# Moving the first batch's loads of u to SyncE's queue and the loads of W1 to ScalarE's

## Chip, cores, metric

One core of a Trainium2 chip runs the whole program. The time is device microseconds of one execution. Runs are fast within 1.5% of the fastest. Medians are quoted for each kernel beside the kernel before on the same chip. A few runs of the kernel before stand far off the rest (1189.03, 1190.59, 1190.67 and 1193.23 among values near 1180.5) and still count as fast, so for effects of one microsecond I read medians, lowest values and traces, and take the ratios only as a bound. Each kernel has one trace, of one run. The "granted clock" of a run or stretch is the share of TensorE's full clock that the profile shows for it.

## The reference

```python
scores = (1.0 / S) * np.matmul(z, z.transpose(0, 2, 1))      # B = 8, S = 3008, d_qk = 64
attn   = np.maximum(scores, 0.0) ** 2
x      = (u * np.matmul(attn, v)).reshape(B * S, 256)
h      = x @ w_in                                             # 256 -> 2048
g      = h * (1.0 / (1.0 + np.exp(-1.702 * h)))
return (g @ w_out).astype(np.float32)                         # 2048 -> 256
```

## The kernel before

Attention goes by query blocks of 512 (six chunks per batch; the last has 448). `attend` yields steps of matmuls, and between them the main loop issues loads, casts and other work by tables of (block, step). Scores go to PSUM (`sc`), ScalarE applies the relu (`rl`, three buffers), VectorE squares (`a`), and SyncE turns squared blocks by DMA transpose (`tt`) so that the upper half of the symmetric score matrix serves for the lower one. `u` arrives as `uq`, VectorE turns it (`ut`), and at a block's end the product with `ut` gives `xt`, the input of the up-projection (`hg`, the product with W1). W1 arrives in four quarters in float32 (`wst`, two buffers), and ScalarE casts each to half precision.

```python
    def load_u(b, i):
        eng = pool if b or i else sp
        ...                                   # four DMAs of 32 partitions each
    def load_w(k):
        if k == 0:
            hold = const.tile([P, 1], F16, name="hold")
            pool.tensor_copy(hold, XT[0, 1][:, 0, :1])
        if k < 4:
            WS[k] = pw.tile([P, NCC, DFF // 4], F32, name="wst", tag="y")
            pool.dma_start(WS[k], moe_w_in...[:, :, k * DFF // 4:(k + 1) * DFF // 4])
        ...
    def cast_w(k):
        act.activation(W1[:, :, k * DFF // 4:(k + 1) * DFF // 4], WS.pop(k), AF.Copy, scale=1.0)
    ...
    TURN0 = {(i, (38, 28)[i] if i < 2 else NJ + 4 if i < NCH - 1 else 12): i for i in range(NCH)}
    LOAD0 = {(1, 14): 2, (2, 12): 3, (2, NJ + 20): 4, (4, 8): 5}
    LOADW = {
        (2, 16): 0, (2, 30): 1, (3, 9): 2, (3, 41): 3, (4, 28): 4, ...
    }
    CASTW = {(3, 8): 0, (3, 40): 1, (4, 8): 2, (4, 14): 3}
```

`TURN0` says where VectorE turns which chunk of u, `LOAD0` where u is loaded, `LOADW` where W1's quarters are, `CASTW` where they are cast; NJ is 24.

Of the kernel before, what the change touches and what calls it, by code (L numbers as in the profile page):

```python
# [10 lines left out]
F16 = mybir.dt.float16  # L11
P = 128
# [3 lines left out]
def kernel(  # L16
# [18 lines left out]
    DFF = moe_w_in.shape[1]  # L35
# [8 lines left out]
    NCC = D // P  # L44
# [11 lines left out]
    dve, act, pe, sp, pool = nc.vector, nc.scalar, nc.tensor, nc.sync, nc.gpsimd  # L56

    const = ctx.enter_context(tc.tile_pool(name="const", bufs=1))
# [18 lines left out]
    ZP, WS = {}, {}  # L77
    late, LATE = [], []
    ZT, V16, UQ, UT, XT, unit, TT = {}, {}, {}, {}, {}, {}, {}
# [41 lines left out]
    def first_cast(g, by_act=False):  # L121
        m = g % CB * CB
        for c in range(2):
            dst, src = ZT["st"][g // CB][:, m:m + CB, c, :], ZT["f"][g // CB][:, m:m + CB, :]
            if by_act:
                act.activation(dst, src, AF.Copy, scale=1.0)  # L126
            else:
                dve.tensor_copy(dst, src)

    def first_zt(g):  # L130

        z2 = ZT["st"][g // CB][:, g % CB * CB:(g % CB + 1) * CB]
        zp = ZP[g] if g in ZP else ps1.tile([P, CB, P], F16, name="zp", tag="ps1")
        for k in range(CB):
            pe.transpose(zp[:, k, :], z2[:, k, :, :], ident)  # L135

        def copies():
            zt = ZT[0][:, g * CB:(g + 1) * CB, :].rearrange("d n p -> d (n p)")
            nb = CB if g < NCH - 1 else CB - 1
            dst = zt[:, :nb * P].rearrange("d (p n) -> d p n", n=nb)  # L140
            src = zp[:, :nb, :].rearrange("d n p -> d p n")
            if g in (0, 2, 3):
                act.activation(dst, src, AF.Copy, scale=1.0)  # L143
            else:
                dve.tensor_copy(dst, src)
            if nb < CB:
                dve.tensor_copy(zt[:, nb * P:], zp[:, nb, :])

        return copies


    def load_z(b):
        ZT[b] = pz.tile([P, NJ, P], F16, name="ZT", tag="ZT")
        for n0 in range(0, NJ, NU):
            zst = pw.tile([P, NU, 2, DQK], F16, name="zst", tag="y")
            full = min(NU, NJ - 1 - n0)
            src = z[b, n0 * P:(n0 + full) * P].rearrange("(n p) d -> p n d", p=P)
            pool.dma_start(zst[:, :full, 0, :], src)
            if full < NU:
                for h in range(2):  # L160
                    pool.dma_start(zst[h * SREM:(h + 1) * SREM, full, 0, :], z[b, S0:S])
            pool.tensor_copy(zst[:, :, 1, :], zst[:, :, 0, :])
            sp.dma_start_transpose(ZT[b][:, n0:n0 + NU], zst.rearrange("p n c d -> p (n c d)"))
# [21 lines left out]
    def width(i):  # L185
        return CH if i < NCH - 1 else LAST

    def load_u(b, i):
        eng = pool if b or i else sp
        n = width(i)  # L190
        uq = pu.tile([P, CH // QW, QW, NCC], F32, name="uq", tag="uq")
        src = u[b, i * CH:i * CH + n].rearrange("(q t) c -> t q c", t=QW)
        for k in range(P // QW):
            cs = slice(k * NCC * QW, (k + 1) * NCC * QW)
            eng.dma_start(uq[k * QW:(k + 1) * QW, :n // QW].rearrange("t q c k -> t q (c k)"), src[:, :, cs])  # L195
        UQ[b, i] = uq

    def turn_u(b, i):
        n = width(i)
        ut = pu.tile([P, NCC, CH // QW, QW], F32, name="ut", tag="ut")  # L200
        UT[b, i] = ut
        dve.transpose(
            ut[:, :, :n // QW, :].rearrange("p k q t -> p q k t"),
            UQ.pop((b, i))[:, :n // QW].rearrange("p q c k -> p q k c"),
        )
# [114 lines left out]
    def full(b):  # L320

        return NCH - 2 if b < B - 1 else NCH - 1
# [106 lines left out]

    def load_w(k):  # L430

        if k == 0:
            hold = const.tile([P, 1], F16, name="hold")
            pool.tensor_copy(hold, XT[0, 1][:, 0, :1])
        if k < 4:
            WS[k] = pw.tile([P, NCC, DFF // 4], F32, name="wst", tag="y")
            pool.dma_start(WS[k], moe_w_in.rearrange("(p k) f -> p k f", k=NCC)[:, :, k * DFF // 4:(k + 1) * DFF // 4])
        else:
            fs = slice((k - 4) * CB, (k - 3) * CB)
            pool.dma_start(W2[:, fs], moe_w_out.rearrange("(fo p) c -> p fo c", p=P)[:, fs])  # L440

    def cast_w(k):
        act.activation(W1[:, :, k * DFF // 4:(k + 1) * DFF // 4], WS.pop(k), AF.Copy, scale=1.0)  # L443
# [197 lines left out]
    def take(b, n):  # L641
        for post_ in scores(b, [queue.pop(0) for _ in range(n)]):
            post_()

    def fill(b):
        assert not queue
        queue.extend(u_ for i in range(NCH) for u_ in pieces(b, i))
# [24 lines left out]
    keep_warm(1)  # L672
    copies()
    ZP[3] = ps1.tile([P, CB, P], F16, name="zp", tag="ps1")
    load_u(0, 1)

    for b in range(B):
        nup = NCH * NFG
        more = b + 1 < B
        sched = SCHED0 if b == 0 else SCHED if more else SCHED_LAST  # L680
        turn, load = (TURN, LOAD) if b else (TURN0, LOAD0)
        head = 0
        for i in range(NCH):
            host = b + 1 if more and i == NCH - 1 else b
            if host > b:
                fill(host)
                LATE.append(host)
            for n, step in enumerate(attend(b, i, b == 0 and i < 2)):
                if b == 0 and i == 0 and n == 5:
                    load_u(0, 0)  # L690
                if b == 0 and i == 0 and n == 2:
                    copies = first_zt(3)
                if b == 0 and i == 0 and n == 3:
                    copies()
                if b == 0 and i == 0 and n in FIRST_CAST:
                    first_cast(FIRST_CAST[n], True)
                if b == 0 and i == 0 and n in FIRST_ZT:
                    first_zt(FIRST_ZT[n])()
                if (i, n) in turn:
                    turn_u(b, turn[i, n])  # L700
                if i == 3 and n in (3, 26) and LAST2:
                    LAST2.pop(0)()
                if (i, n) in load:
                    load_u(b, load[i, n])
                if b == 0 and (i, n) in CASTW:
                    cast_w(CASTW[i, n])
                if b == 0 and (i, n) in LOADW:
                    load_w(LOADW[i, n])
                if more and (i, n) == (NCH - 2, 2 if b else 16):
                    load_z(b + 1)  # L710
                if b == 0 and i == NCH - 1 and n in (8, 30, 42):
                    wsums.pop(0)()
                take(host, sched[i].get(n, 0))
                if i == full(b) and n >= HEAD and (n - HEAD) * LAGY // (2 * NJ - 10) >= head and head < LAGY:
                    up_group(b, head)
                    head += 1
                step()
        late.sort(key=lambda t: t[0])
        if more:
            for i in range(2):  # L720
                load_u(b + 1, i)
            for n0 in range(0, NJ, VB):
                load_v(b + 1, n0)
        prods = products(b)
        for q in range(head, nup):
            if more and q in (head + 14, head + 20):
                k = int(q == head + 20)
                turn_u(b + 1, k)
                load_u(b + 1, k + 2)
            up_group(b, q)  # L730
            if b == 0 and q == head + 3:
                wsums.pop(0)()
            product(b, *prods.pop(0))
            if q >= 30 and q % 2 and late:
                late.pop(0)[1]()
        steps = [lambda kp=kp: product(b, *kp) for kp in prods]
        for step in steps:
            step()
            for sum_ in [SUMS.pop(0) for _ in range(min(len(SUMS), 1 + (len(SUMS) > 4)))]:
                sum_()  # L740
            for _, turn_it in [late.pop(0) for _ in range(min(len(late), 1 + (len(steps) < 10)))]:
                turn_it()
        LATE.clear()
        if more:
            while late:
                late.pop(0)[1]()
            take(b + 1, 2)
# [30 lines left out]
```

## Time and profile before

| | kernel before |
|---|---|
| median of 6 runs | 1180.49 us (1180.28 to 1183.42) |
| span of the profiled run | 1178.7 us |
| TensorE time lost against its pace, 40 to 60 and 60 to 80 us | 0.50 and 0.93 us |

The prediction shows the page's main lines. The columns of the timeline are start, length, engine, line, operation, tiles and shapes, count, idle time before it and what ended that. In the timeline (start, length, engine, line, operation, tiles and shapes, count, idle time before it and what ended that), VectorE turns u of chunk 3 with no wait:

```profile
58.81 0.63 DVE L270 TENSOR_TENSOR a<-rl 128x896 f16<-128x896 f16 x1 [0.18 <-ACT rl L256]
59.36 1.24 DVE L202 STREAM_TRANSPOSE ut<-uq 128x1024 f32<-128x1024 f32 x1
```

And TensorE goes from block 3 into the first up-projection (`hg`) without a hole:

```profile
62.53 1.15 PE L358 MATMUL o<-a,V 64*128 64x512 f16 x6
63.52 1.03 PE L399 MATMUL hg<-xt,W 128*128 128x512 f16 x4
```

The trace gives for each transfer when it was issued and when it landed. "Hole" is, throughout, the start of one matmul less the start of the one before and less its regular pace (0.216 us for a 512-column matmul of 128 rows, half that for one of a pair of 64 rows). In the lines, SPq and ACTq are the instructions by which SyncE and ScalarE issue transfers, and `<-` in the brackets names what ended the idle time.

### The profile page before, as it was taken

How to read it: one execution, taken by the hardware profiler on the slowest of the kernel's cores; microseconds unless marked ns; L12 is line 12 of the kernel's file. 1: busy time of each engine (PE TensorE's matmuls, PEld its weight loads, DVE VectorE, ACT ScalarE, POOL GpSimd, SP SyncE). 2: the span in 40 equal slices, each digit the busy share in tenths (PEclk: the TensorE clock that was granted, in tenths of full speed). 3: DMA queues.
4: the chain of work that ended last, by engine and by line, in shares of the span. 5: the costliest groups of instructions: out<-in, count | busy, mean ns of one | idle time of the engine just before them, and what ended most of it. 6: DMA issues, size and time to landing. Idle time of an engine off the chain costs nothing.

```text
span 1178.7 us, 23495 instructions
## 1 busy us (share of the span) xinstructions
PE 1172.5 (99%) x9238; PEld 667.2 (57%) x9238; DVE 870.7 (74%) x1455; ACT 849.6 (72%) x1033; POOL 222.1 (19%) x313
## 2 busy tenths in 40 slices
PE   9999999999999999999999999999999999999998
PEld 3446664466644675446654467544674446744566
DVE  6779866878758786587875878658786587764776
ACT  7888874688746887478864787647876478772785
POOL 5243101231012310132101431014100241001000
PEclk9999999999999999999999999999999999999999
DMA  9998679877698677976879668896578965796023
GB/s 226 217 120 125 133 116 160 91 112 135 106 156 100 108 135 130 150 91 95 147 128 149 94 93 157 139 137 94 94 135 135 141 106 97 127 158 127 1 37 73
DMA packets 449696, 143.66 MB, mean 122 GB/s; under 512 B 414640, under 2 KB 443056, under 8 KB 449584
## 3 DMA queue, kind: packets, MB, share of 16 engines
q1 hardware_dynamic: 392160, 99.80, 51.2%
q0 software_dynamic: 56064, 41.04, 23.1%
q8 instruction: 72, 1.18, 0.4%
q10 hardware_dynamic: 1360, 1.31, 0.4%
q14 instruction: 40, 0.33, 0.1%
HBM read 60.29 MB, written 24.64 MB: 72 GB/s over the span
## 4 chain that ended last, share of the span: by engine, by line
PE 99%; ACT 1%; issue 0%; DVE 0%
PE o L358 40%; PE hg L399 27%; PE st L523 23%; PE sc L235 6%; PE st L526 1%; PE yp L497 1%; PE w L99 0%; ACT rl L256 0%; ACT W L443 0%; ACT gf L407 0%; PE zp L135 0%; ACT ZT L143 0%; ACT zst L126 0%; DVE y L544 0%; DVE nil L75 0%
## 5 line engine op out<-in xcount | busy, mean ns | idle before, releaser
L407 ACT ACTIVATE gf<-hg 128x1024 f32<-128x1024 f32 (+1 forms) x384 | 385.5, 1004 | 113.6 <-PE hg L399 98.3
L256 ACT ACTIVATE rl<-sc 128x1024 f16<-128x1024 f32 (+1 forms) x301 | 287.5, 993 | 145.4 <-PE sc L235 101.2
L358 PEld LDWEIGHTS <-V 64*128 64x128 f16 (+1 forms) x4052 | 217.7, 94 | 253.9 <-issue 11.8
L399 PE MATMUL hg<-xt,W 128*128 128x512 f16 (+1 forms) x1408 | 354.6, 374 | 0.2
L358 PE MATMUL o<-a,V 64*128 64x512 f16 (+3 forms) x2240 | 296.0, 368 | 0.0
L411 DVE TENSOR_SCALAR gt<-gf 128x1024 f16<-128x1024 f32 (+1 forms) x288 | 203.0, 705 | 114.0 <-ACT gf L407 112.8
L195 POOL DMA_DIRECT2D uq<-in_u_dram x188 | 125.2, 674 | 751.8 <-PE sc L235 527.5
L270 DVE TENSOR_TENSOR a<-rl 128x1024 f16<-128x1024 f16 (+1 forms) x266 | 177.6, 670 | 112.3 <-ACT rl L256 111.0
L358 PE MATMUL o<-tt,V 64*128 64x512 f16 (+1 forms) x1510 | 232.2, 377 | 0.0
L399 PEld LDWEIGHTS <-W 128*128 128x128 f16 x1536 | 149.4, 98 | 125.6 <-issue 2.6
L523 PEld LDWEIGHTS <-WT 128*128 128x128 f16 x1472 | 139.1, 98 | 45.1
L523 PEld LDWEIGHTS <-W 128*128 128x128 f16 x1104 | 104.7, 98 | 32.2
L235 PE MATMUL sc<-ZT 64*128 64x512 f16 (+3 forms) x688 | 115.5, 357 | 0.5 <-ACT ZT L143 0.3
L409 ACT ACTIVATE gt<-gf 128x1024 f16<-128x1024 f32 (+1 forms) x96 | 98.9, 1030 | 3.0
L540 ACT ACTIVATE y<-st 128x256 f32<-128x256 f32 x192 | 70.8, 369 | 35.7 <-PE st L523 29.2
L523 PE MATMUL st<-gt,WT 128*128 128x256 f16 (+1 forms) x736 | 91.9, 268 | 0.0
L523 PE MATMUL st<-s,WT 128*128 128x256 f16 (+1 forms) x736 | 90.8, 268 | 0.0
L523 PE MATMUL st<-gt,W 128*128 128x256 f16 (+1 forms) x736 | 90.8, 268 | 0.0
L544 DVE SCALAR_TENSOR_TENSOR y<-st,y 128x256 f32<-128x256 f32 (+1 forms) x144 | 57.7, 407 | 24.3 <-ACT y L540 11.7
L375 DVE TENSOR_TENSOR xt<-o,ut 128x512 f16<-128x512 f32 x80 | 51.3, 683 | 28.5 <-PE o L358 28.5
L477 DVE TENSOR_TENSOR s<-s,gt 128x1024 f16<-128x1024 f16 (+1 forms) x96 | 63.7, 663 | 1.1
L475 DVE TENSOR_TENSOR s<-gt 128x1024 f16<-128x1024 f16 (+1 forms) x96 | 63.3, 660 | 0.0
(59 smaller groups left out, 668.5 us busy)
## 6 DMA issues: line engine op xcount, KB each, us to landing
uq<-in_u_dram POOLq DMA_DIRECT2D x156, 128.0 KB, 3.6
out_dram<-yo SPq DMA_DIRECT2D x156, 128.0 KB, 2.8
V<-in_v_dram POOLq DMA_DIRECT2D x35, 256.0 KB, 6.4
tt<-a SPq DMA_TRANSPOSE x232, 3.4
uq<-in_u_dram POOLq DMA_DIRECT2D x32, 112.0 KB, 5.4
out_dram<-yo SPq DMA_DIRECT2D x28, 96.0 KB, 6.0
wst<-in_moe_w_in_dram POOLq DMA_DIRECT2D x4, 512.0 KB, 6.2
vst<-in_v_dram SPq DMA_DIRECT2D x3, 512.0 KB, 5.4
```

What stands on the lines that cost most here:

```text
L195: eng.dma_start(uq[k * QW:(k + 1) * QW, :n // QW].rearrange("t q c k -> t q (c k)"), src[:, :, cs])
L235: pe.matmul(sc[:, r, :q1 - q0], zt[h, 2 * kp + r, :], zt[h].rearrange("d n p -> d (n p)")[:, q0:q1], start=True, stop=True,)
L256: act.activation(rl[:, :, :n], sc[:, :, :n], AF.Relu, scale=csc)
L270: dve.tensor_tensor(a[:, :, :n], rl[:, :, :n], rl[:, :, :n], ALU.mult)
L358: ins = pe.matmul(acc[c][:, :n], V16[b][h, j].rearrange("p (c k) -> p k c", k=NCC)[:, c], weights(b, i, j)[h], start=(k, m) == first[c], s ...
L399: pe.matmul(hg[:, e, :n], W1[:, c, ff * P:(ff + 1) * P], XT[b, i][:, c, :n], start=(c == 0), stop=(c == NCC - 1),)
L407: act.activation(gf[:, :, :n], hg[:, :, :n], AF.Gelu_apprx_sigmoid, scale=1.0 / FSC)
L409: act.activation(g, gf[:, :, :n], AF.Copy, scale=FSC)
L411: dve.tensor_scalar(g, gf[:, :, :n], FSC, None, ALU.mult)
L477: dve.tensor_tensor(s_, ST[b, k, "S1", h], a11, ALU.subtract)
L523: pe.matmul(bank, right[:, ff], lhs()[:, f], start=first, stop=last, skip_group_check=True)
L540: act.activation(y[:, c, :, o], bank, AF.Copy, scale=1.0 / FSC)
```

## The change

Its intent: in the first batch Pool issues no loads of u or W1. SyncE issues u of all chunks and ScalarE the four quarters of W1; the small copy that only held Pool back goes.

```diff
     def load_u(b, i):
-        eng = pool if b or i else sp
+        eng = pool if b else sp
...
     def load_w(k):
-        if k == 0:
-            hold = const.tile([P, 1], F16, name="hold")
-            pool.tensor_copy(hold, XT[0, 1][:, 0, :1])
         if k < 4:
             WS[k] = pw.tile([P, NCC, DFF // 4], F32, name="wst", tag="y")
-            pool.dma_start(WS[k], ...)
+            act.dma_start(WS[k], ...)
...
     ZP[3] = ps1.tile([P, CB, P], F16, name="zp", tag="ps1")
-    load_u(0, 1)
...
-                if b == 0 and i == 0 and n == 5:
-                    load_u(0, 0)
+                if b == 0 and i == 0 and n in (5, 24):
+                    load_u(0, n // 24)
```

More of the change, by code (lines that the diff above doesn't have):

```diff
@@ L430, in load_w @@
     def load_w(k):
-        if k == 0:
-            hold = const.tile([P, 1], F16, name="hold")
-            pool.tensor_copy(hold, XT[0, 1][:, 0, :1])
         if k < 4:
             WS[k] = pw.tile([P, NCC, DFF // 4], F32, name="wst", tag="y")
-            pool.dma_start(WS[k], moe_w_in.rearrange("(p k) f -> p k f", k=NCC)[:, :, k * DFF // 4:(k + 1) * DFF // 4])
+            act.dma_start(WS[k], moe_w_in.rearrange("(p k) f -> p k f", k=NCC)[:, :, k * DFF // 4:(k + 1) * DFF // 4])
         else:
```

## The prediction

> **What bounds the kernel now.** First the engines' busy time and the chain of waits on the profile page, to learn whether any engine but one matters:
>
> ```profile
> PE 1172.5 (99%) x9238; PEld 667.2 (57%) x9238; DVE 870.7 (74%) x1455; ACT 849.6 (72%) x1033; POOL 222.1 (19%) x313
> ...
> PE 99%; ACT 1%; issue 0%; DVE 0%
> ```
>
> TensorE is busy 1172.5 of 1178.7 us, and the chain that ended last runs through it for 99%. So a gain must come from TensorE's remaining holes, and a loss must open a new hole in it. Second, the list of waits, where the largest wait of all is just the one that the change takes away:
>
> ```profile
> POOL uq L195 <- PE sc L235: 527.5, 14, 66.1
> POOL wst L437 <- PE sc L235: 13.1, 2, 8.3
> POOL wst L437 <- ACT W L443: 3.0, 1, 3.0
> PE w L99 <- DVE nil L75: 1.2, 1, 1.2
> PE sc L235 <- ACT ZT L143: 0.3, 1, 0.3
> ```
>
> The reader should see that the first three belong to Pool, which nobody on the chain waits for, and that TensorE's own two waits sum to 1.5 us, both before 6 us. Third, only the first batch changes, so the busy times by stage there (columns: stretch, length, then busy us of TensorE, weight loads, VectorE, ScalarE, Pool, granted clock, DMA share, GB/s):
>
> ```profile
> 38.00:52.00 14.00, 14.00 (x134) 6.37 (x130) 10.04 (x16) 11.79 (x13) 4.23 (x7) 1.00 1.21 223
> 52.00:64.00 12.00, 12.00 (x111) 5.91 (x106) 9.29 (x17) 11.61 (x15) 1.81 (x3) 1.00 1.12 198
> 64.00:80.00 16.00, 15.76 (x73) 6.81 (x72) 11.15 (x19) 13.99 (x14) 6.48 (x9) 1.00 1.02 117
> ```
>
> Here are the two things that can hurt: ScalarE is 97% busy in 52 to 64 us (11.61 of 12.00), and the DMA engines are at or over a full share in all of it. Busy hides small delays, so I also took the starts of consecutive matmuls from the trace and compared them with their regular pace (0.216 us for a full 512-column one, half of that for each of a pair of 64-row ones). What is lost over 20 us is 5.2 us in 0 to 20 (start-up), 2.3 in 20 to 40 (a 0.2 us step at each change between 64-row and 128-row tiles), 0.5 in 40 to 60 and 0.9 in 60 to 80; later it is about 0.35 on average. The single holes in 40 to 80 us are 0.25 at 54.2, 0.21 at 56.7, and 0.28 each at 68.9 and 72.0 us. The last two wait for the casts of W1's third and fourth quarters on ScalarE; those quarters landed long before or (68.90 against 71.41 us for the cast) 2.5 us before. No load is what is waited for.
>
> **The Trainium skill.** "Trainium Kernel Development and Optimization", Key Constraints: DMAs from the SP, ACT and POOL queues run on the same 16 DMA engines, and spreading them saves only the sequencer's issue time. That agrees with the shares above, over 1.0 already: the move changes no bytes. "DMA: Bandwidth & Descriptors", Anatomy of one DMA: a semaphore wait happens on the issuing sequencer before dispatch, not in the DMA engine. So a load put on ScalarE makes ScalarE wait; the trace shows it on Pool, whose third W1 load stood 3.0 us until the cast of the first. "Perfetto Trace Analysis", DVE / Act Engine Instruction: compute instructions go into a wait queue and an execution FIFO while the sequencer goes on. So an issue of about 0.5 us can lie beneath an ACTIVATE of 1.0 us; nothing in the kernel before shows this in the middle of a stage.
>
> **The change, part by part.** (1) Removed from Pool: 20 u loads of 0.65 us, one 0.19 us copy (`hold`) and 4 W1 loads of 0.71 us, 16 us in all. The chain has none of it, so it is worth 0.
>
> (2) Added to SyncE: 20 u loads (five chunks of four). The four already there took 0.48 us each:
>
> ```profile
> 14.19 2.16 SPq L195 DMA_DIRECT2D uq<-in_u_dram  x4
> 16.45 45.97 SPq L298 DMA_TRANSPOSE tt<-a  x20
> ```
>
> Each chunk is thus 2.2 us more of a queue that stands in order and is nearly always occupied in 16 to 62 us; four chunks fall into or beside it, 8.6 us. Against it stands the slack of the transposes: from the trace, the tile for key chunk 2 of block 0 landed at 26.7 and is first read by TensorE at 38.9; the others have 8.3, 18.0, 14.5, 8.4, 14.4, 13.4, 13.5, 10.1 and 10.7 us. The queue also had gaps (19.2 to 25.6 us, waiting for VectorE), which swallow the first moved chunk, and Pool's loads no longer compete with it at 17 to 30 us. Delays of 2 to 6 us fit; 0 on the path. The tightest u is chunk 3: VectorE turned it at 59.36; I put its new issue at about 54 and its landing at 57.5 to 60.5. VectorE may wait up to about 1 us; ScalarE has three `rl` buffers and would feel it only after about 1.5 us.
>
> (3) Added to ScalarE: 4 issues of about 0.5 us (its two v loads took 0.47 and 0.57). Where they stand decides. In the changed program the first comes after the ACTIVATE that ended at 42.12; the next begins at 44.11 after idling 2.0 us, so it is free. The second comes about 46.9, beneath or behind an ACTIVATE. The slack of TensorE there (start of its next scores less the end of the ACTIVATE that frees their PSUM tile) is 0.39 to 0.71 us. Free or nearly. The third and the fourth each follow a cast:
>
> ```profile
> 44.11 8.53 ACT L256 ACTIVATE rl<-sc 128x1024 f16<-128x1024 f32 x9 [2.00 <-PE sc L235]
> 52.54 1.05 ACT L443 ACTIVATE W<-wst 128x1024 f16<-128x1024 f32 x1
> 53.48 8.18 ACT L256 ACTIVATE rl<-sc 128x1024 f16<-128x1024 f32 x9
> 61.56 1.05 ACT L443 ACTIVATE W<-wst 128x1024 f16<-128x1024 f32 x1
> 62.51 0.91 ACT L256 ACTIVATE rl<-sc 128x896 f16<-128x896 f32 x1
> 63.31 0.49 ACT L251 ACTIVATE rl<-sc 128x384 f16<-128x384 f32 x1
> 63.82 1.28 ACT L407 ACT_TABLE_LOAD   x1
> ```
>
> The fourth load waits in the program for the end of the cast just ahead of it, at 62.61. With the issue, the next ACTIVATE begins at about 63.15 in place of 62.51. It frees the PSUM tile of the first up-projection, which started at 63.52 with 0.10 us of slack: TensorE loses about 0.64 - 0.10 = 0.5 us. The third waits for the cast that ended at 53.59, while the next ACTIVATE already runs to 54.5; beneath it there is room for the issue, if its other wait is over.
>
> (4) That other wait is the new thing. In both programs the transfers of SyncE and ScalarE share eight completion semaphores in rotation, and each issue waits until the earlier user of its semaphore has landed. In the changed program one semaphore is used in turn by W1's first quarter (ScalarE), the first half of the transpose for block 1 and key chunk 4 (SyncE), the third quarter (ScalarE) and the fourth. So the in-order queues now wait for each other. First quarter: issued about 42.2 and landing, at the 5.5 to 7.3 us of the four before, at 48 to 49.5. The transpose, which went out at 46.15 before, now goes at 48.5 to 50 and lands, at its 4.9 us of before, at 53.4 to 54.8. The third quarter is ready to go at 53.6. ScalarE stands between 0 and 1.2 us; the slack of TensorE there is 0.05 to 0.07 us, so nearly all passes on. I take 0.4. The fourth needs the third landed, at about 54.2 + 6.3 = 60.5, before its turn at 62.6: fits with 2 us.
>
> Sum: 0 - 0 + 0.5 (fourth load) + 0.4 (semaphore) + 0.1 (second) = +1.0, less at most 0.3 if a hole at 54 to 57 closes, for which I take 0.2. From the median 1180.45 that is 1181.2 us. The other seven batches stay: their orders on each engine are the same.
>
> **Rivals.** A: Pool's descriptors or its late loads were in the way of the transposes or of VectorE, and the early stage gets quicker. For it: DMA share 1.08 to 1.23 in 16 to 52 us and transposes that took up to 8.9 us to land. Against it: TensorE never waited for a transpose. At most the holes of 40 to 60 us, 0.5 us: 1180.0. B: the cross-wait bites, ScalarE stands 2 us or more at 54, u of chunk 3 comes late, and both pass to TensorE: +3 to +4, 1184. It needs the first quarter to land at 51 or later; the slowest W1 load before took 7.3 us, which gives 49.5. C: ScalarE's issues are hidden wholly and the semaphore wait is met: 1180.4. I hold C and my sum about equally likely, B at one in eight.
>
> **Range and chances.** All rivals lie within 0.3% of the time before, whose own three runs spread over 3 us (1180.28 to 1183.42). 1179.6 to 1184.2 should hold it 8 times in 10. For 2% TensorE would have to lose or gain 24 us; it has only about 9 us of holes in the first 80 us, most of them start-up, so faster is all but excluded, and slower by so much would take ScalarE or SyncE standing for 24 us.
>
> **What would show it.** Pool has no load before about 69 us. The first W1 issue on ScalarE stands in an idle stretch near 42; the fourth near 62.6 and TensorE's first up-projection begins 0.5 us later against its neighbours. If the transpose named above goes out right after W1's first quarter lands, step 4 is right; if ScalarE's third issue starts more than 1 us after the cast's end, B is. Wrong would be: TensorE waiting for a transposed tile, VectorE waiting over 1.5 us for u, or any change after 100 us.

## The result

The changed kernel takes 1182.08 us in the median of 6 runs (1181.40 to 1184.67), the kernel before 1180.49: 1.6 us more. The ratio of the fast runs is 1.0012, with a 95% interval of 0.9999 to 1.0025. (Ratios are the mean time of one kernel's fast runs over that of the other's of the same rounds, so not quite the ratio of the medians.) The profiled run was the slowest of the six, at 1184.67; its span is 1182.9 us, 4.2 us over the one before.

The page's first lines and chain, after:

```profile
PE 1173.7 (99%) x9238; PEld 667.8 (56%) x9238; DVE 871.2 (74%) x1455; ACT 849.6 (72%) x1033; POOL 205.4 (17%) x288
...
PE 97%; ACT 1%; DMA 1%; DVE 0%; issue 0%; SPq 0%; DVEq 0%; ACTq 0%
```

Pool lost 16.7 us of work, as planned, and TensorE's share of the chain fell from 99 to 97%: a transfer and SyncE's queue have come into it. By stage (columns as in the prediction):

```profile
52.00:64.00 12.00, 11.39 (x104) 5.55 (x101) 6.92 (x12) 9.95 (x12) 0.00 (x0) 1.00 1.15 195
64.00:80.00 16.00, 14.24 (x57) 5.77 (x57) 9.94 (x16) 12.64 (x14) 2.44 (x3) 0.89 0.97 150
```

TensorE lost 0.6 us in the first of these and 1.5 more than before in the second, where its granted clock fell to 0.89. The lists of waits, SyncE's own and that of the other engines, name the new ones (who waited, for whom, us in all, times, longest):

```profile
SPq L298 <- DMA wst<-in_moe_w_in_dram: 6.4, 1, 6.4
DVE ut L202 <- DMA uq<-in_u_dram: 3.6, 1, 3.6
ACT rl L256 <- DVE a L270: 2.2, 1, 2.2
PE hg L399 <- ACT rl L256: 2.1, 1, 2.1
```

Read upwards, TensorE's first up-projection waited for ScalarE's relu to free its PSUM tile, ScalarE for VectorE to free an `rl` buffer, VectorE for u of chunk 3; and earlier SyncE had stood 6.4 us for W1's first quarter. The timelines show the same by the clock, first SyncE, then VectorE, ScalarE and TensorE:

```profile
36.76 17.96 SPq L298 DMA_TRANSPOSE tt<-a  x8
54.77 3.75 SPq L195 DMA_DIRECT2D uq<-in_u_dram  x4
```

```profile
58.53 0.63 DVE L270 TENSOR_TENSOR a<-rl 128x896 f16<-128x896 f16 x1 [0.18 <-ACT rl L256]
62.71 1.25 DVE L202 STREAM_TRANSPOSE ut<-uq 128x1024 f32<-128x1024 f32 x1 [3.56 <-DMA uq<-in_u_dram]
```

```profile
53.20 1.02 ACT L256 ACTIVATE rl<-sc 128x1024 f16<-128x1024 f32 x1
53.33 0.56 ACTq L434 DMA_DIRECT2D wst<-in_moe_w_in_dram  x1
...
61.27 1.05 ACT L440 ACTIVATE W<-wst 128x1024 f16<-128x1024 f32 x1
62.35 0.55 ACTq L434 DMA_DIRECT2D wst<-in_moe_w_in_dram  x1
64.56 0.92 ACT L256 ACTIVATE rl<-sc 128x896 f16<-128x896 f32 x1 [2.23 <-DVE a L270]
```

```profile
62.24 1.15 PE L358 MATMUL o<-a,V 64*128 64x512 f16 x6
65.52 1.86 PE L399 MATMUL hg<-xt,W 128*128 128x512 f16 x4 [2.13 <-ACT rl L256]
67.18 1.06 PE L358 MATMUL o<-a,V 128*128 128x512 f16 x2
```

The hole is 2.30 us. After it four matmuls took 1.86 us where they took 1.03 before: eight of them in a row were 0.43 us apart, twice the pace, which is 1.65 us more. In the stretch from 66 to 69 us the granted clock is 0.52:

```profile
66.00:69.00 3.00, 3.00 (x9) 1.03 (x8) 2.18 (x6) 2.18 (x2) 0.00 (x0) 0.52 1.23 192
```

So this profiled run lost 2.30 + 1.65 = 3.95 us of its 4.2. (What is left is small and lies elsewhere: TensorE began 0.3 us earlier than before, and lost 0.4 at about 1084 us, where it waited 0.2 us for a transposed tile. The second run of this kernel, e1, has no such loss; e3, e6 and e12 have 0.3 to 0.7 us at the same matmul.)

The Trainium skill, "TensorE: Matmul & The Clock Gate", What's actually happening, says that the array falls to half its clock after at least one idle window of about 3.4 us, and that the windows are free-running: they do not start with the kernel. The traces agree with the half clock and with the windows, and not with the length of idling. The half clock lasted from 65.45 to 68.86 us, 3.41 us, and began 61.44 us after the clock's first change, both in this run and in e1; in the other traces the next change came after 1170.77 or 1174.18 us. These are 18, 343 and 344 times 3.413 us, so the changes stand on a grid whose place differs from run to run. In the grid's window from 62.04 to 65.45 TensorE was idle for 2.05 us in all (by the profile's modelled ends), not for the whole of it; in e1 it was 2.27. Idle sums of 1.84 us in one window (e2) and of 1.76 (e10, whose hole was longer but lay across two windows, 1.11 and 1.76) were not followed by half clock. So in these four traces what tells is how much idle time falls into one window; no experiment moved it on purpose.

The five other runs, 2 to 3 us faster and with a mean clock of 0.999 or 1.000 against 0.998, presumably paid the hole and not the half clock.

### The profile page after: what moved, and what is told of

It is laid out like the page before. It is cut to its first block, busy times and chain, and to the rows that moved or that the text cites. A ratio compares the mean times of both kernels' runs of the same rounds, so it can differ in the third digit from the quotient of the medians.

```text
span 1182.9 us, 23487 instructions
## 1 busy us (share of the span) xinstructions
PE 1173.7 (99%) x9238; PEld 667.8 (56%) x9238; DVE 871.2 (74%) x1455; ACT 849.6 (72%) x1033; POOL 205.4 (17%) x288
## 3 DMA queue, kind: packets, MB, share of 16 engines
q10 hardware_dynamic: 2448, 3.41, 1.1%
## 4 chain that ended last, share of the span: by engine, by line
PE 97%; ACT 1%; DMA 1%; DVE 0%; issue 0%; SPq 0%; DVEq 0%; ACTq 0%
PE o L358 39%; PE hg L399 27%; PE st L520 23%; PE sc L235 6%; PE st L523 1%; PE yp L494 1%; ACT rl L256 0%; DMA uq<-in_u_dram 0%; DMA tt<-a 0%; PE w L99 0%; SPq L195 0%; DVE a L270 0%; ACT W L440 0%; ACT gf L407 0%; DVE xt L375 0%
## 5 line engine op out<-in xcount | busy, mean ns | idle before, releaser
L411 DVE TENSOR_SCALAR gt<-gf 128x1024 f16<-128x1024 f32 (+1 forms) x288 | 200.0, 694 | 115.0 <-ACT gf L407 112.6
L195 POOL DMA_DIRECT2D uq<-in_u_dram x168 | 111.1, 668 | 752.0 <-PE sc L235 543.1
```

The costliest lines, as they stand in the source:

```text
L195: eng.dma_start(uq[k * QW:(k + 1) * QW, :n // QW].rearrange("t q c k -> t q (c k)"), src[:, :, cs])
L411: dve.tensor_scalar(g, gf[:, :, :n], FSC, None, ALU.mult)
```

## The experiments

All ran with five timed rounds. The theory at the start: SyncE stands for W1's first quarter through a shared completion semaphore, so u of chunk 3 comes late, and the delay passes down through VectorE and ScalarE to TensorE. R1: SyncE's queue is too long with u, semaphores or not. R2: ScalarE's own issues are the cost. In the table, "hole" is the one ahead of the first up-projection (0.00 in the kernel before), of the profiled run, and "u 3" is when the last load of chunk 3's u landed.

| run | median us | before | difference | by lowest values | hole us | u 3 landed |
|---|---|---|---|---|---|---|
| changed kernel | 1182.08 | 1180.49 | +1.6 | +1.1 | 2.30 | 62.5 |
| e1_again | 1182.34 | 1180.75 | +1.6 | +1.6 | 2.47 | 62.6 |
| e2_w_alone | 1183.79 | 1180.75 | +3.0 | +2.9 | 0.75, and 2.35 at 55 us | 56.0 (from Pool) |
| e3_u_alone | 1181.30 | 1180.75 | +0.5 | 0.0 | 0.31 | 61.5 |
| e4_turn_late | 1181.52 | 1180.75 | +0.8 | +1.2 | 0.74 | 62.2 |
| e6_u3_early | 1181.52 | 1180.86 | +0.7 | +0.8 | 1.42 | 41.4 |
| e7_w0_early | 1181.24 | 1180.86 | +0.4 | +0.7 | 0.74 | 55.9 |
| e8_cast_early | 1181.14 | 1180.86 | +0.3 | +0.1 | 0.42 | 62.7 |
| e10_cast_only | 1182.29 | 1180.86 | +1.4 | +1.2 | 3.03 | 63.5 |
| e12_both | 1180.50 | 1181.33 | -0.8 | +0.3 | 0.00 | 55.3 |
| e17_pool_cast | 1179.59 | 1181.33 | -1.7 | -0.7 | 0.00 | 55.7 |

The kernel before was disturbed in the last call (five of its eleven runs over 1182; its lowest is 1180.20), so e12 and e17 are better held against its lowest. All ratios' intervals contain 1: the smallest and the largest ratio are 0.9977 (0.9944 to 1.0010, e17) and 1.0027 (0.9995 to 1.0059, e2). No ratio is clear of the noise; the causes below rest on the holes in the traces, with the medians beside them.

### e1_again: the changed kernel, unaltered

> The changed kernel once more, unaltered. All theories: +0.8 to +2.0 us over the kernel before in the fast runs. What it is for: a second profile, because the first was of the slowest of six runs (1184.67 against a median of 1182.08). My theory (SyncE stands for W1's first quarter through a shared completion semaphore, so u of chunk 3 comes late, so VectorE, ScalarE and TensorE stand one after the other): u of chunk 3 lands again after 60 us, VectorE waits 1.5 to 3.6 us for it, TensorE's first up-projection is 1 to 2.3 us late; in a run near the median without the slow matmuls of half pace that followed the hole in the first profile. Rival R2 (the fourth W1 issue on ScalarE itself costs it): the hole is 0.5 to 0.7 us and VectorE's wait does not matter.

The same 1.6 us, and the same picture: VectorE waited 3.7 us, the hole was 2.47 us, and half pace followed it again in the profiled run (1184.28 us, clock 0.998). One unprofiled run of the six was also at 1184.44 with that clock. So the first profile was no accident, but it shows the dearer of two outcomes.

### e2_w_alone: W1 from ScalarE, u left on Pool

```diff
-        eng = pool if b else sp
+        eng = pool if b or i else sp
+    load_u(0, 1)
-                if b == 0 and i == 0 and n in (5, 24):
-                    load_u(0, n // 24)
+                if b == 0 and i == 0 and n == 5:
+                    load_u(0, 0)
```

> W1's quarters from ScalarE, u of all chunks but 0 still from Pool. My theory: u of chunk 3 comes from Pool's own queue in time, so at most the half microsecond of the fourth issue is left: 0.0 to +0.7 us over before. Rival R1 (SyncE's queue is too long with the u loads, semaphores or not): 0.0. Rival R2 (ScalarE's issues are the cost): +1.2 to +2.0 us, all of the loss.

This part alone costs 3.0 us, more than the whole change: my figure, R1's and R2's all failed. ScalarE's timeline shows why. Its third W1 issue stood from the cast's end to 56.12, and the relu behind it waited for a transpose:

```profile
53.58 1.02 ACT L256 ACTIVATE rl<-sc 128x1024 f16<-128x1024 f32 x1
56.12 0.55 ACTq L434 DMA_DIRECT2D wst<-in_moe_w_in_dram  x1
56.77 1.73 ACT L256 ACTIVATE rl<-sc 128x896 f16<-128x896 f32 x2 [2.17 <-DMA tt<-a]
```

With fewer transfers on SyncE the rotation of the eight semaphores falls differently: here the third quarter shares one with the first half of the transpose for block 2 and key chunk 4, which landed at 56.04. That is rival B of the prediction, in another program. 2.35 + 0.75 us of holes make the 3.0, to 0.1.

### e3_u_alone: u from SyncE, W1 left on Pool

```diff
+        if k == 0:
+            hold = const.tile([P, 1], F16, name="hold")
+            pool.tensor_copy(hold, XT[0, 1][:, 0, :1])
-            act.dma_start(WS[k], ...)
+            pool.dma_start(WS[k], ...)
```

> u of all chunks from SyncE, W1's quarters and the small copy still from Pool. My theory: no semaphore is shared with a W1 load, SyncE does not stand for one, u of chunk 3 lands by about 58 us and VectorE does not wait more than 1 us: 0.0 to +0.4 us over before. R1: u of chunk 3 lands after 60 us here as well, +1.2 to +2.0 us. R2: 0.0.

All three figures failed, mine by little: +0.5 us, and VectorE waited 1.6 us, where I had allowed 1, though no semaphore is shared with W1:

```profile
61.52 1.25 DVE L202 STREAM_TRANSPOSE ut<-uq 128x1024 f32<-128x1024 f32 x1 [1.57 <-DMA uq<-in_u_dram]
```

So the semaphore is not the whole reason for the late u. The issue times show what is. The third quarter of W1 is 512 KB, each of the four loads of u 128 KB:

| run | third quarter issued | u 3 issued | u 3 landed |
|---|---|---|---|
| e3 | 54.39 | 53.40, 54.02, 54.58, 55.11 | 56.5, 57.1, 60.5, 61.5 |
| e8 | 54.12 | 53.71, 54.33, 54.88, 55.54 | 56.7, 60.6, 62.4, 62.7 |
| changed | 53.33 | 54.77, 55.51, 56.17, 57.86 | 61.4, 61.8, 62.1, 62.5 |
| e7 | 53.85 | 50.87, 51.49, 52.02, 52.55 | 54.2, 54.7, 55.5, 55.9 |

A load of u issued ahead of the third quarter lands in 3.0 to 3.5 us, one issued behind it in 4.7 to 7.5. The fourth quarter parts the next chunk's loads in the same way: in e4 the load issued at 62.47, 0.11 us ahead of it, took 3.4 us and the next one 6.3. So what decides is whether u of chunk 3 is issued before that quarter; SyncE's standing matters only through this.

### e4_turn_late: VectorE turns u of chunk 3 later

```diff
-    TURN0 = {(i, (38, 28)[i] if i < 2 else NJ + 4 if i < NCH - 1 else 12): i for i in range(NCH)}
+    TURN0 = {(i, (38, 28)[i] if i < 2 else NJ + 20 if i == 3 else NJ + 4 if i < NCH - 1 else 12): i for i in range(NCH)}
```

> The changed kernel with VectorE's turning of u chunk 3 put 16 steps later in block 3 (it is needed only at the block's end). u of chunk 3 lands as late as before, but VectorE squares the scores ahead of it. My theory and R1: the hole of TensorE shrinks to at most the 0.5 to 0.6 us of the fourth issue, so 0.0 to +0.9 us over before. R2: the loss stays, +1.2 to +2.0 us.

u lands as late as in the changed kernel (62.2), and the hole falls from 2.47 to 0.74 us; of the time, half of the loss goes by medians (+0.8 in place of +1.6), but only 0.3 us by lowest values (1181.37 against 1181.70). R2, by which the loss would have stayed, does not explain the shorter hole. What is left is the fourth W1 issue behind its cast, on ScalarE and then on TensorE:

```profile
62.58 0.55 ACTq L434 DMA_DIRECT2D wst<-in_moe_w_in_dram  x1
63.22 0.92 ACT L256 ACTIVATE rl<-sc 128x896 f16<-128x896 f32 x1 [0.68 <-PE o L358]
```

```profile
64.19 1.02 PE L399 MATMUL hg<-xt,W 128*128 128x512 f16 x4 [0.58 <-ACT rl L256]
```

The releaser in brackets misleads here: the issue ended 0.1 us before that relu, and nothing else did. The hole of 0.74 us is this issue's.

### e6_u3_early: u of chunk 3 ahead in the queue

```diff
-    LOAD0 = {(1, 14): 2, (2, 12): 3, (2, NJ + 20): 4, (4, 8): 5}
+    LOAD0 = {(1, 14): 2, (1, NJ + 14): 3, (2, NJ + 20): 4, (4, 8): 5}
```

> The changed kernel with u of chunk 3 issued some 22 steps earlier (block 1, step 38), so that in SyncE's queue it stands ahead of the transposes that wait for W1's first quarter. It should be issued near 37 us and land before 43 us; VectorE does not wait for it. SyncE still stands for W1's first quarter (6 us), behind u. If the late u is what opens the hole beyond the fourth issue: +0.6 to +1.1 us over before, as with the later turn (the fourth issue behind its cast stays, 0.6 to 0.8 us; it waits here for the second half of the transpose for block 2 and key chunk 4, which may add up to 0.5). If SyncE's standing costs by another way (transposes that come late): +1.2 to +2.0 as in the changed kernel.

u landed at 41.4, VectorE did not wait for it, and +0.7 is left, within what the late-u theory gave. SyncE still stood 7.3 us for W1's first quarter, and TensorE waited for no late tile in this stretch. But the rotation moved again: ScalarE's fourth issue now waited for a transpose that landed at 63.16, and the hole is 1.42 us in the profiled run. (That transpose went out at 56.33, 3.0 us later than in the changed kernel; whether SyncE's standing made it so late is not shown.)

```profile
63.24 0.55 ACTq L434 DMA_DIRECT2D wst<-in_moe_w_in_dram  x1
63.88 0.92 ACT L256 ACTIVATE rl<-sc 128x896 f16<-128x896 f32 x1 [1.36 <-DMA tt<-a]
```

### e7_w0_early: the first quarter 16 us earlier

```diff
-        (2, 16): 0, (2, 30): 1, (3, 9): 2, (3, 41): 3, ...
+        (1, 2): 0, (2, 30): 1, (3, 9): 2, (3, 41): 3, ...
```

> The changed kernel with W1's first quarter put on ScalarE's queue some 16 us earlier (block 1, step 2; its buffer is long free). The next user of its semaphore is then a transpose that goes out near 31 us, so SyncE should not stand 6.4 us in 43 to 49 us; the second quarter is then what the fourth u load of chunk 3 waits for. If the shared semaphore is what makes u of chunk 3 late: it is issued near 48 to 50 us, lands by 56 us, VectorE does not wait, +0.6 to +1.0 us over before is left (the fourth issue). If the length of SyncE's queue and the busy DMA engines make it late (as the run with u alone suggests, where it landed at 61.5 without any shared semaphore): it lands after 59 us again and the loss stays at +1.2 to +2.0.

SyncE does not stand for W1 any more, u of chunk 3 goes out at 50.87, ahead of the third quarter, and VectorE turns it without a wait (SyncE's queue, then VectorE):

```profile
37.28 13.54 SPq L298 DMA_TRANSPOSE tt<-a  x8
50.87 2.17 SPq L195 DMA_DIRECT2D uq<-in_u_dram  x4
```

```profile
59.59 1.24 DVE L202 STREAM_TRANSPOSE ut<-uq 128x1024 f32<-128x1024 f32 x1
```

In the changed kernel the same eight transposes took until 54.71. The hole is 0.74 us, the fourth issue's, as in e4; the time, +0.4 us, is below the 0.6 to 1.0 that I expected. This run moved the quarter's traffic as well as its semaphore, so it does not say how much of those 3.9 us each made; e3, where SyncE issued u at 53.40 with no shared semaphore but the quarter's traffic in the way, puts about 1.4 us of them with the semaphore, and e8, where it is shared but SyncE stood only 3.3 us for it, issued u at 53.71: it varies from run to run.

### e8_cast_early and e10_cast_only: the fourth issue not behind a cast

```diff
-    CASTW = {(3, 8): 0, (3, 40): 1, (4, 8): 2, (4, 14): 3}
+    CASTW = {(3, 8): 0, (3, 30): 1, (4, 8): 2, (4, 14): 3}
```

This line alone is e10; e8 has e4's edit besides.

> The changed kernel with the later turn of u chunk 3 (as in the run before this one) and, besides, the cast of W1's second quarter 10 steps earlier in block 3, so that the fourth W1 issue no longer stands right behind it. If the two parts are u (0.8 us) and the fourth issue behind the cast (0.8 us), both are gone: 0.0 to +0.5 us over before, TensorE's hole ahead of the first up-projection under 0.35 us. If something else is left: +0.7 or more.

> The changed kernel with only the cast of W1's second quarter 10 steps earlier; the turn of u chunk 3 stays where it was. In the changed kernel's profile ScalarE stood until 64.56 us for VectorE, well beyond the end of the fourth issue at 62.9, so the two delays lie beside each other and not one behind the other. Then taking away the fourth issue alone gains nothing: +1.2 to +2.0 us. If they add up: +0.6 to +1.0.

e8 is left with +0.3 us and a hole of 0.42, a little over the 0.35 expected. In both runs the fourth issue took a new place in the rotation, behind the last load of u of chunk 3: in e8 that landed at 62.74, the issue followed at 62.82, and ScalarE's next relu began only at 63.47. So the fourth issue is out from behind the cast but not free, and this is what is left. e10 gains next to nothing (+1.4) though its issue is not behind the cast either: ScalarE stands for VectorE in any case. (It is not a clean test of 0.7 us, as u landed 1.0 us later than in the changed kernel.)

```profile
65.51 0.92 ACT L256 ACTIVATE rl<-sc 128x896 f16<-128x896 f32 x1 [3.43 <-DVE a L270]
```

So the two losses lie beside each other, and taking away the shorter alone gains nothing. e10 also has the longest hole, 3.03 us, and its profiled run was not at half pace afterwards, while the changed kernel's was after 2.30.

### e12_both and e17_pool_cast: a version without the losses

e12 has the edits of e7 and e10. e17 has e7's and lets Pool, which the change left idle, do the casts:

```diff
-        act.activation(W1[:, :, k * DFF // 4:(k + 1) * DFF // 4], WS.pop(k), AF.Copy, scale=1.0)
+        pool.tensor_copy(W1[:, :, k * DFF // 4:(k + 1) * DFF // 4], WS.pop(k))
-    CASTW = {(3, 8): 0, (3, 40): 1, (4, 8): 2, (4, 14): 3}
+    CASTW = {(2, 24): 0, (3, 12): 1, (3, 44): 2, (4, 2): 3}
```

> The changed kernel with both remedies that leave the turn of u alone: W1's first quarter some 16 us earlier (SyncE does not stand for it) and the cast of the second quarter 10 steps earlier (the fourth issue not behind a cast). If the two named causes are all of the loss: -0.3 to +0.5 us against before, TensorE's hole ahead of the first up-projection under 0.3 us. If not: +0.7 or more.

> The changed kernel with W1's first quarter 16 us earlier and the four casts of W1 moved from ScalarE to Pool, which has nothing else to do there, each at the place where its quarter should have landed. The holes that were in the kernel before too, two of 0.28 us at the third and fourth casts and 0.25 us after the first, should close, and the fourth issue stands behind no cast: -0.9 to -0.2 us against before if Pool's casts (1.8 us each by the 0.9 us that its casts of half the size took) are ready in time; +0.5 or more if TensorE waits for the fourth quarter, which landed at 67.6 us in the run with the earlier first quarter and is needed at about 72.

e12 is back at the time before (1180.49 to 1181.22; the lowest of before is 1180.20), with no hole: the two causes are all of the loss. (Its trace is 0.7 us longer than that of the kernel before, all of it at the matmul near 1081 us that was named above.) e17 runs 1179.48 to 1180.27. Five of its six runs lie below 1180.15, the lowest run of the kernel before in any call, and against 1180.5, where most of those runs lie, its median is 0.9 us less. Its trace shows the same: TensorE's loss in 40 to 80 us is 0.58 us, 1.43 before (0.19 and 1.05 at exactly 0.216 us), because the holes at ScalarE's casts are gone. In its stretch from 64 to 80 us TensorE is busy throughout, and Pool's casts took 1.0 to 1.5 us, not the 1.8 that I had estimated:

```profile
64.00:80.00 16.00, 16.00 (x76) 7.24 (x75) 12.16 (x18) 11.89 (x13) 5.42 (x7) 1.00 1.38 144
```

```profile
61.28 1.52 POOL L440 CAST W<-wst 128x1024 f16<-128x1024 f32 x1 [9.91 <-DMA wst<-in_moe_w_in_dram]
66.01 1.04 POOL L440 CAST W<-wst 128x1024 f16<-128x1024 f32 x1 [3.22 <-DVE gt L411]
```

## Why the prediction was right, and where not

**The size and the sign.** 1181.2 was forecast and 1182.08 measured, inside the range; slower by 0.8 forecast, 1.6 measured. That the number came so near is partly luck. Of the terms that were priced, none is what the changed kernel pays: the fourth load (0.5) lies beneath a longer wait, the semaphore wait at ScalarE (0.4) and the second load (0.1) did not show, and the holes at 54 to 57 us for which 0.2 was taken off stayed (0.25 and 0.21). What it pays is the term taken as 0, and the prediction's own sign of being wrong, "VectorE waiting over 1.5 us for u", came true with 3.6 us. Rival B was right in its second half (u late, passed to TensorE) and wrong in its first (ScalarE standing at 54). That Pool's work was worth nothing held: no chain had it. In the other seven batches TensorE kept its pace but for the 0.4 us near 1084 us, which e1 does not have.

**The fourth load, 0.5 us.** Right as a cost. It shows alone in e4 and e7: a hole of 0.74 us, of which the list gives 0.58 as wait, against 0.5 worked out. In the changed kernel itself it ended at 62.90, beneath the wait for VectorE until 64.5, and costs nothing of its own.

**The first and second load, 0.0 and 0.1.** Right: they were issued at 40.87 and at 45.34, and no hole followed either. The first came 1.3 us earlier than forecast, beneath an ACTIVATE and not in the idle stretch after it. That an issue can lie beneath an ACTIVATE, which the prediction drew from the Trainium skill, "Perfetto Trace Analysis", DVE / Act Engine Instruction, held for the third load too: 53.33 to 53.89, within an ACTIVATE from 53.20 to 54.22, and the next ACTIVATE was not late.

**The semaphore, 0.4 us at ScalarE.** The mechanism was right and its place wrong. The transpose went out at 49.28, 0.06 us after the first quarter landed at 49.22, as described (the quarter, issued early, took 8.35 us and not 5.5 to 7.3, and so landed in the forecast range all the same); but the transpose landed at 52.55, before the cast's end, so ScalarE did not wait (its issue is at 53.33, within the relu). It was SyncE that stood, 6.4 us, and the prediction charged that with nothing. e2 and e6 show the case at ScalarE that the prediction priced, in other rotations, at 2.35 and about 0.7 us.

**The step that failed: "VectorE may wait up to about 1 us; ScalarE ... would feel it only after about 1.5 us", hence 0 for u.** The issue time was well estimated (about 54; 54.77). The landing was not: 57.5 to 60.5 against 62.5, because the loads fell behind W1's third quarter on the DMA engines, and each took 4.7 to 6.6 us: from the first issue to the last landing it was 7.8 us, where 3.5 to 6.5 had been assumed. VectorE waited 3.6 us and ScalarE 2.2. This term, taken as 0, is worth 0.8 to 1.2 us in the median (the changed kernel's +1.6 less the +0.8, +0.7 and +0.4 of e4, e6 and e7, which take VectorE's wait away in three ways), and 2.3 in the profiled run.

**What I did not think of.** A hole can cost more than its length: 1.65 us of half pace followed the 2.30 in the profiled run, and as much followed in e1's.

**What stays open.** How the 3.9 us by which SyncE came late to u divide between the semaphore and the quarter's traffic; and how long the hole is in the unprofiled runs, which the traces do not show (the median's +1.6 suggests 1.6 us without half pace).

## What to carry to other kernels

Putting loads on another engine's queue moves waits as well as issues: where the queues share a few completion semaphores in rotation, two in-order queues begin to wait for each other, and any added or removed transfer deals these waits anew. Before such a move, list for each semaphore who uses it in turn, and for each load what large transfer will stand ahead of it when it is really issued; here a load of 128 KB took 4.7 to 7.5 us behind one of 512 KB in place of 3.0 to 3.5. When two delays lie side by side, removing the shorter shows nothing and removing the longer shows only the difference, so remove both before dropping either theory.

## What the Trainium skill lacked or had wrong

- "Trainium Kernel Development and Optimization", Key Constraints, says what spreading DMAs over queues saves (the sequencer's issue time). No page tells what it can cost: a queue stood 6.4 us (SyncE, changed kernel) and ScalarE over 2 us (e2) for a transfer of the other through a shared completion semaphore.
- "DMA: Bandwidth & Descriptors", neither in its Rules for kernel authors nor elsewhere, gives a time for small loads beside a large one: 128 KB loads from SyncE landed in 3.0 to 3.5 us when issued ahead of a 512 KB load and in 4.7 to 7.5 us behind it.
- "TensorE: Matmul & The Clock Gate", Why this matters for your kernels, allows gaps up to about 3 us between bursts of matmuls. Here an idle time of 2.13 us was followed by eight matmuls at half pace, and one of 2.87 us (e10) was not: the length of the gap alone does not tell. In the four traces above it was the idle time within one window of 3.41 us: 2.05 and 2.27 us were followed by half clock, 1.76 and 1.84 were not.
